# A first unit with an order of its own, and a running state kept whole: a gated-linear-attention and two mixture-of-experts layers on one core

## The chip, the cores and the metric

The kernel runs on one NeuronCore of one Trainium2 chip. The metric is device time in microseconds (us) of one execution; lower is better. Three executions of the kernel before took 754.09, 754.20 and 754.47 us, median 754.20 us.

## The reference

Three layers, one after the other. The attention keeps one 48x48 state for each of 2 batches x 8 heads; its decay `alpha` differs by row of the state and by position.

```python
# attention: q, k, v, alpha are [2, 8, 768, 48]
for t in range(S):
    state = alpha[:, :, t, :, None] * state + einsum('bhd,bhe->bhde', k[:, :, t], v[:, :, t])
    y[:, :, t] = einsum('bhd,bhde->bhe', q[:, :, t], state)
x = y.transpose(0, 2, 1, 3).reshape(1536, 384)
# first mixture: 4 experts, every row through all of them
for e in range(4):
    out += p[:, e:e + 1] * (relu(x @ w1[e]) @ w2[e])       # w1[e]: 384x1024, w2[e]: 1024x384
# second mixture: 8 experts, each row through the two that its noisy logits choose
```

## The kernel before

**Units and groups.** The 2 x 768 positions are cut into seven units (`sizes`: 128, 256, 256, 128, 256, 256, 256). Two heads form a pair (`p`, 96 of 128 partitions; a head has 48 rows at partition 0 or 64), and a chunk `c` is 128 positions. A group is two (pair, chunk) tiles side by side: two pairs of one chunk in a unit of 128, two chunks of one pair in a unit of 256. Groups are counted through all units by `k`: 0 and 1 are the first unit's, 2 to 5 the second's.

**Stages of a group.** `decays` transposes alpha on TensorE and makes with scans on VectorE the running products `A` and the reversed ones `F` (tile `suffix`). `keys` and `queries` transpose k and q and multiply them by `F` and `A`; ScalarE makes `G` from `K`. `keys_back` transposes `K` back, and ScalarE copies it out as `Kn`. `scores` multiplies G with Q into two PSUM banks, `sc0` and `sc1` (for two groups at once after the first unit), and VectorE masks each into `M`. `states` multiplies `Kn` with v into one bank, again `sc0`, and VectorE updates the state `St` from it: the result for a pair is 96x96, and only its two 48x48 blocks on the diagonal belong to the state. `outputs` adds the state's part and M's part in one PSUM bank; ScalarE copies it out rounded (`xh`), and VectorE takes the rest (`xl`). For the first unit the output goes to `x32` unsplit.

**Order.** `plan` gives each stage of a group a step: `base` plus an offset, where `base` rises by 2 for the first two groups and by 3 afterwards. Within a step the stages run by a fixed rank. Engines execute in the order in which the program was written. Wherever `IDLE` says so, `busy` puts matmuls of ones in front of a stage; nothing reads what they compute. The names `tr` (2 banks), `g` (4), `sc0` and `sc1` (1 each) are PSUM banks: a matmul that wants one waits until its last reader is done.

**Beside the attention** runs the first expert of the first mixture (`moe1(0, ...)`). `drive` takes a piece of it (`hidden` for one f, or two f of `product`) and then as many steps of the attention as keep both level. It starts with the first unit's 128 rows when the first `rows_at[0]` steps are written, which is 9. For these rows `hidden` uses whole float32 weights (L491, `raw` 4 to 7); afterwards each weight is a rounded part and a rest, with three matmuls (L495 to L497, L510 to L512). The rounded parts are made on ScalarE (L144) and the rests on GpSimd (L145), a group of weights in a piece.

**Loads** are issued by SyncE, in the order of the program, into one queue: the first unit's alpha, k and q in halves, its v, the second unit's alpha, k and q, weights 4 and 5, the second unit's v, weights 6 and 7, and then the second weights of the expert.

Of the kernel before, what the change touches and what calls it, by code (L numbers as in the profile page):

```python
# [28 lines left out]
def kernel(  # L29
# [203 lines left out]
    for i in range(2):  # L233
        t = apool.tile([P, BM, H, 2, D], F32, name=f"v{i}")
        nc.gpsimd.memset(t[:, :, :, 1, :], 0.0)
        V.append(t)
# [6 lines left out]
    def load_unit(u, names, p0=0, p1=HP):  # L243

        if u >= NU:
            return
        b, h0 = divmod(starts[u], S)
        hs = slice(2 * p0, 2 * p1)
        for nm in names:
            for c in range(sizes[u] // P):  # L250
                frm = src[nm][b, hs, h0 + c * P:h0 + (c + 1) * P, :].rearrange("h p d -> p h d")
                if nm == "v":
                    nc.sync.dma_start(V[u % 2][:, c, hs, 0], frm)
                    continue
                nc.sync.dma_start(inputs(nm, u)[:, c, hs, :D], frm)
# [9 lines left out]
    suffix = []  # L265
    for i in range(2):
        t = apool.tile([P, UM], F32, name=f"suffix{i}")
        nc.gpsimd.memset(t, 1.0)
        suffix.append(t)
    St = []  # L270
    for p in range(HP):
        t = apool.tile([P, BM + 1, 2 * D], F32, name=f"S{p}")
        nc.gpsimd.memset(t, 0.0)
        St.append(t)
# [4 lines left out]
    def attention(u):  # L279
# [8 lines left out]
        def slot(c):  # L288
            return (starts[u] // P + c) % (BM + 1)
# [17 lines left out]
        def decays(g):  # L307
            A = group(g, "A")
            st[g, "rc"] = rc = apool.tile([P, BM], F32, tag="rc", name="rc", bufs=3)
            st[g, "F"] = F = next(suffixes)  # L310
# [9 lines left out]
        def keys(g):  # L320
            K, G = group(g, "K", 2), group(g, "G")
            nc.vector.tensor_mul(K, transposed("k", g), st[g, "F"])
# [41 lines left out]
        def states(g):  # L364
# [4 lines left out]
            for i, p, c in updated(g):  # L369
                nc.tensor.matmul(t[:, i * 2 * D:(i + 1) * 2 * D].rearrange("x (j d) -> x j d", j=2), Kn[:, i, :],  # L370
                                 V[u % 2][:, c, 2 * p:2 * p + 2, 0, :], start=True, stop=True)
# [12 lines left out]

        def outputs(g):
            Q = st[g, "Q"]
            t = ps("g", 4)
            for i, (p, c) in enumerate(groups[g]):
                y = t[:2 * D, at(i)]
                inter = not (first and c == 0)  # L390
                if inter:
                    nc.tensor.matmul(y, St[p][:, slot(c), :], Q[:, at(i)], start=True, stop=False)  # L392
                two = V[u % 2][:, c].rearrange("x h k d -> x (h k d)")
                for j in range(2):
                    nc.tensor.matmul(y, two[:, (4 * p + j) * D:(4 * p + j + 2) * D], st[g, j][:, i, :],  # L395
# [21 lines left out]
            for y, r, d, to in pieces:  # L417
                nc.vector.tensor_sub(xl[r, d, to], y, xh.bitcast(F32)[r, d, to])  # L418
# [20 lines left out]
        def outputs_(g):  # L439
            outputs(g)  # L440
            if g == len(groups) - 1:
                load_unit(u + 2, "v")

        return len(groups), paired, (outputs_, states, keys, scores, keys_back, queries_, decays_), parted

    suffixes = itertools.cycle(suffix)

    rows_at = {}
    NEAR = 2

    IDLE = {(2, 0): 5, (1, 0): 5, (2, 1): 2, (1, 1): 4, (2, 2): 4, (1, 2): 2, (0, 0): 1, (0, 1): 1, (0, 2): 1}

    def plan():
        at = {}
        base = 0
        k = 0
        for u in range(NU):
            n, paired, stages, parted = attention(u)
            for g in range(n):
                near = k < NEAR  # L460
                offs = (5, 4, 1, 3, 3, 2, 0) if near else (7 if g % 2 or not paired else 9, 6, 1, 4, 3, 2, 0)
                for order, (stage, off) in enumerate(zip(stages, offs)):
                    at.setdefault(base + off, []).append((order, k, stage, g))
                end = base + (5 if near else 7)
                base += 2 if near else 3
                k += 1
            rows_at[u] = end + 2
            if u == 0:
                at.setdefault(end + 6, []).append((7, k, parted, 0))
# [4 lines left out]
    def stream():  # L474
        for i in range(max(steps) + 1):
            for order, k, f, g in sorted(steps.get(i, ()), key=lambda z: z[:2]):
                busy(IDLE.get((order, k), 0))
                f(g)
            yield
# [5 lines left out]
    def hidden(e, f, hx, lx, t0, n, H_):  # L485
        t = ps("g", 4)
        for kd in range(KD):
            if e == 0 and n == P:
# [13 lines left out]
        nc.vector.scalar_tensor_tensor(hl[:, :n], t[:, :n], 0.0, hh.bitcast(F32)[:, :n],  # L502
                                       op0=OP.max, op1=OP.subtract)
        H_[f] = (hh, hl)

# [10 lines left out]
    def moe1(e, t0, n, then=None):  # L516
        H_ = {}
        last = t0 + n == N
        for f in range(KF):
            hidden(e, f, xh, xl, t0, n, H_)  # L520
            if last and f % FG == FG - 1:
                W.done.add((e, 1, f // FG))
            yield
        if then is not None:
# [43 lines left out]
    psm = const.tile([P, NB], F32, name="psm")  # L568

    def probabilities():  # L570
        nc.vector.reduce_sum(psm, prob, axis=AX.X)
        nc.vector.tensor_scalar(psm, psm, 1e-9, None, op0=OP.add)
# [6 lines left out]
    for what in ("a", "k", "q", 4, 5, "v", 6, 7, 0, 1, "p", 2, 3):  # L579
# [18 lines left out]
    for _ in until(rows_at[0]):  # L598
        if now >= 15 and W.n_prep < 4:
            W.prep()  # L600
# [578 lines left out]
```

## Time and profile before

| | |
|---|---|
| median of three runs | 754.20 us |
| the profiled execution | 754.46 us, of which its span is 751.9 us |
| TensorE (PE) busy | 740.4 us, 98% |
| VectorE (DVE) busy | 358.0 us, 48% |
| ScalarE (ACT) busy | 246.2 us, 33% |
| GpSimd (POOL) busy | 163.4 us, 22% |
| chain of work that ended last | PE 92%, DVE 5% |

The span is what the trace covers; the 2.6 us beside it are the start and the end of the execution. Shares are over the whole span; the attention lasts for the first quarter of it, and there VectorE's share is far higher than in the table. A matmul's record runs to the modelled end of its pipeline, so two records overlap, and what the engine sustains is seen in the distance of their starts.

### The profile page before, as it was taken

How to read it: one execution, taken by the hardware profiler on the slowest of the kernel's cores; microseconds unless marked ns; L12 is line 12 of the kernel's file. 1: busy time of each engine (PE TensorE's matmuls, PEld its weight loads, DVE VectorE, ACT ScalarE, POOL GpSimd, SP SyncE). 2: the span in 40 equal slices, each digit the busy share in tenths (PEclk: the TensorE clock that was granted, in tenths of full speed). 3: DMA queues.
4: the chain of work that ended last, by engine and by line, in shares of the span. 5: the costliest groups of instructions: out<-in, count | busy, mean ns of one | idle time of the engine just before them, and what ended most of it. 6: DMA issues, size and time to landing. Idle time of an engine off the chain costs nothing.

```text
span 751.9 us, 11931 instructions
## 1 busy us (share of the span) xinstructions
PE 740.4 (98%) x4618; PEld 701.3 (93%) x4618; DVE 358.0 (48%) x868; ACT 246.2 (33%) x485; POOL 163.4 (22%) x177
## 2 busy tenths in 40 slices
PE   9999999999999999999999999999999999999997
PEld 5888999999898989989899999999999999999996
DVE  5888666664222122222212336367844564554551
ACT  2543323233312041210314314333534354444430
POOL 2440000001510032100134100011251524424331
PEclk9999999999999999999999999999999999999999
DMA  9945212100640012100114200011755554655620
GB/s 190 200 117 106 53 32 44 22 1 23 175 103 0 1 43 85 42 1 1 33 61 124 67 25 19 23 43 36 244 183 155 178 165 144 204 161 159 200 71 31
DMA packets 98254, 66.96 MB, mean 89 GB/s; under 512 B 57834, under 2 KB 94757, under 8 KB 98193
## 3 DMA queue, kind: packets, MB, share of 16 engines
q1 hardware_dynamic: 93168, 52.02, 25.8%
q0 software_dynamic: 5024, 14.13, 6.0%
q8 instruction: 38, 0.62, 0.3%
q14 instruction: 24, 0.19, 0.1%
HBM read 56.69 MB, written 9.82 MB: 88 GB/s over the span
## 4 chain that ended last, share of the span: by engine, by line
PE 92%; DVE 5%; ACT 1%; DMA 1%; issue 1%; POOL 0%; POOLq 0%; DVEq 0%
PE g L495 13%; PE g L496 13%; PE g L497 13%; PE g L510 10%; PE g L512 10%; PE g L511 10%; PE g L1019 3%; PE g L1021 3%; PE g L1020 3%; PE g L395 3%; PE tr L297 2%; PE sc L355 2%; PE tr L953 1%; PE g L192 1%; PE g L392 1%; PE sc L678 1%
## 5 line engine op out<-in xcount | busy, mean ns | idle before, releaser
L501 ACT ACTIVATE hh<-g 128x384 fp32r<-128x384 f32 (+8 forms) x200 | 96.7, 485 | 263.7 <-PE g L497 250.9
L502 DVE SCALAR_TENSOR_TENSOR hl<-g,hh 128x384 fp32r<-128x384 f32 (+8 forms) x200 | 109.1, 549 | 147.6 <-ACT hh L501 143.7
L510 PE MATMUL g<-w2h,hl 128*128 128x384 f32 x464 | 161.5, 348 | 0.0
L512 PE MATMUL g<-w2h,hh 128*128 128x384 f32 x464 | 156.4, 337 | 0.0
L511 PE MATMUL g<-w2l,hh 128*128 128x384 f32 x464 | 156.4, 337 | 0.0
L495 PE MATMUL g<-xh,w1l 128*128 128x512 f32 (+2 forms) x360 | 125.9, 350 | 0.0
L496 PE MATMUL g<-xl,w1h 128*128 128x512 f32 (+2 forms) x360 | 123.6, 343 | 0.1
L497 PE MATMUL g<-xh,w1h 128*128 128x512 f32 (+2 forms) x360 | 123.4, 343 | 0.0
L510 PEld LDWEIGHTS g<-w2h,hl 128*128 128x128 f32 x464 | 87.3, 188 | 1.0
L511 PEld LDWEIGHTS g<-w2l,hh 128*128 128x128 f32 x464 | 87.4, 188 | 0.3
L512 PEld LDWEIGHTS g<-w2h,hh 128*128 128x128 f32 x464 | 87.2, 188 | 0.0
L145 POOL TENSOR_TENSOR w1l<-raw,w1h 128x768 fp32r<-128x768 f32 x16 | 29.2, 1840 | 266.0 <-ACT w1h L144 266.0
L539 DVE SCALAR_TENSOR_TENSOR acc<-g,prob,acc 128x384 f32<-128x384 f32 x36 | 22.2, 618 | 116.9 <-PE g L512 116.9
L495 PEld LDWEIGHTS g<-xh,w1l 128*128 128x128 f32 x360 | 67.8, 188 | 6.0
L495 PE MATMUL g<-xth,w1l 128*128 128x256 f32 (+6 forms) x216 | 73.4, 340 | 0.0
L496 PEld LDWEIGHTS g<-xl,w1h 128*128 128x128 f32 x360 | 67.9, 189 | 5.8 <-DVE xl L418 0.3
L497 PEld LDWEIGHTS g<-xh,w1h 128*128 128x128 f32 x360 | 67.8, 188 | 5.7
L496 PE MATMUL g<-xtl,w1h 128*128 128x256 f32 (+6 forms) x216 | 71.3, 330 | 0.0
L497 PE MATMUL g<-xth,w1h 128*128 128x256 f32 (+6 forms) x216 | 71.4, 330 | 0.0
L144 ACT ACTIVATE w2h<-raw 128x768 fp32r<-128x768 f32 x44 | 36.8, 845 | 35.1 <-issue 23.0
L971 POOL DMA_INDIRECT out_dram<-yo,si_c x26 | 26.1, 1004 | 85.9 <-DVE yo L970 79.8
L1019 PE MATMUL g<-hh,w2l 128*128 128x432 f32 (+4 forms) x120 | 43.3, 361 | 0.0
(194 smaller groups left out, 1047.6 us busy)
## 6 DMA issues: line engine op xcount, KB each, us to landing
raw<-in_moe_w_dram SPq DMA_DIRECT2D x76, 384.0 KB
raw<-in_moe_w_dram SPq DMA_DIRECT2D x16, 288.0 KB
v<-in_v_dram SPq DMA_DIRECT2D x12, 192.0 KB
out_dram<-zero SPq DMA_DIRECT2D x1, 2304.0 KB
x2d<-acc SPq DMA_DIRECT2D x12, 192.0 KB
x_a<-in_alpha_dram SPq DMA_DIRECT2D x20, 96.0 KB
x_k<-in_k_dram SPq DMA_DIRECT2D x18, 96.0 KB
x_q<-in_q_dram SPq DMA_DIRECT2D x18, 96.0 KB
```

The costliest lines, as they stand in the source:

```text
L144: nc.scalar.activation(hi, r, AF.Copy)
L145: (nc.gpsimd if e < E1 or own else nc.vector).tensor_sub(lo, r, hi.bitcast(F32))
L495: nc.tensor.matmul(t[:, :n], wl, hx[:, kd, t0:t0 + n], start=(kd == 0), stop=False)
L496: nc.tensor.matmul(t[:, :n], wh, lx[:, kd, t0:t0 + n], start=False, stop=False)
L497: nc.tensor.matmul(t[:, :n], wh, hx[:, kd, t0:t0 + n], start=False, stop=(kd == KD - 1))
L501: nc.scalar.activation(hh[:, :n], t[:, :n], AF.Relu)
L502: nc.vector.scalar_tensor_tensor(hl[:, :n], t[:, :n], 0.0, hh.bitcast(F32)[:, :n], op0=OP.max, op1=OP.subtract)
L510: nc.tensor.matmul(t[:m, :DM], hl[:, o:o + m], wh, start=(f == 0), stop=False)
L511: nc.tensor.matmul(t[:m, :DM], hh[:, o:o + m], wl, start=False, stop=False)
L512: nc.tensor.matmul(t[:m, :DM], hh[:, o:o + m], wh, start=False, stop=(f == KF - 1))
L971: nc.gpsimd.indirect_dma_start(out=parts_of_out[s], out_offset=bass.IndirectOffsetOnAxis(ap=SLOT[e * SB + s][2][:n, e * SB + s:e * SB + s ...
L1019: nc.tensor.matmul(t[:, :n], wl, hh[:, :n], start=(f == 0), stop=False)
```

## The change

Five things change.

- The running state is kept whole. A tile `full` holds each pair's 96x96 result with its off-diagonal blocks. Each update is one instruction of 96 columns on all partitions instead of two of 48x48; the first chunk's is a copy on ScalarE. Two ScalarE copies then move the diagonal blocks into `St`, whose other blocks stay zero. These copies, and the rests `xl`, are put on a list (`later`) and written at the end of the step.
- `plan` has tables by stage: own steps and ranks for groups 0 and 1, and for the others `states` one step earlier, with a rank behind `queries`, and `scores` ahead of `keys`. In the first unit the making of the state (`keys_back`, `states`) comes after the outputs, and the transposes of the first q and the second alpha go to a `g` bank.
- `IDLE` holds 10 matmuls of ones instead of 25; the ten at the very start stay. The first expert starts after 5 steps instead of 9.
- Queues: weights 4 are loaded ahead of the second unit's k and q, and weights 6 ahead of its v, which so comes after three groups of weights instead of two. v is laid out as (head, zeros, head) for a pair, so that a load is two DMAs of half the size and the zeros are half as many. The third unit's v is loaded after the first unit's states.
- One `suffix` tile instead of two, `A` in two buffers instead of three; the sum of the probabilities gets its small constant from a tile. In `hidden`, for 128 rows, VectorE's `hl` is written after the attention's steps of that piece.

```diff
-                    nc.sync.dma_start(V[u % 2][:, c, hs, 0], frm)
+                    for j in range(2):
+                        nc.sync.dma_start(V[u % 2][:, c, p0:p1, 2 * j], frm[:, j::2])
...
-            t = ps("tr", 2)
+            t = ps("g", 4) if u == 0 and (nm, g) in (("q", 0), ("a", 1)) else ps("tr", 2)
...
-            for i, p, c in updated(g):
+            o = t[:, :BM * 2 * D].rearrange("x (i e) -> x i e", i=BM)
+            if first and UB == 1:
+                ps_ = slice(groups[g][0][0], groups[g][-1][0] + 1)
+                nc.scalar.activation(full[:, ps_, 0], o, AF.Copy)
+            else:
...
+                        prev = full[:, p, c - 1 if c else sizes[u - 1] // P - 1]
+                        nc.vector.scalar_tensor_tensor(full[:, p, c], prev, A[:, i * P + P - 1:i * P + P], o[:, i],
+                                                       op0=OP.mult, op1=OP.add)
...
+            def diagonal():
                 for j in range(2):
                     rows = slice(64 * j, 64 * j + D)
                     cols = slice(j * D, (j + 1) * D)
-                    o = t[rows, i * 2 * D + j * D:i * 2 * D + (j + 1) * D]
-                    to = St[p][rows, slot(c + 1), cols]
-                    if first and c == 0:
-                        nc.vector.tensor_copy(to, o)
-                    else:
-                        nc.vector.scalar_tensor_tensor(to, St[p][rows, slot(c), cols],
-                                                       A[rows, i * P + P - 1:i * P + P], o,
-                                                       op0=OP.mult, op1=OP.add)
+                    nc.scalar.activation(St[rows, ps_, new, cols], full[rows, ps_, :n, cols], AF.Copy)
+
+            later.append(diagonal)
...
-    IDLE = {(2, 0): 5, (1, 0): 5, (2, 1): 2, (1, 1): 4, (2, 2): 4, (1, 2): 2, (0, 0): 1, (0, 1): 1, (0, 2): 1}
+    NEAR = ({"decays": (0, 0), "keys": (0, 1), "queries": (0, 2), "scores": (1, 0), "outputs": (2, 0),
+             "keys_back": (4, 7), "states": (5, 5)},
...
+    ORDER = {"outputs": 0, "scores": 1, "keys": 2, "keys_back": 3, "queries": 4, "states": 5, "decays": 6}
...
+    IDLE = {("scores", 0): 2, ("outputs", 0): 3, ("scores", 1): 2, ("outputs", 1): 1, ("keys", 2): 2}
...
-        base = 0
+        base = 3
...
                 f(g)
+            while later:
+                later.pop(0)()
             yield
...
-    for what in ("a", "k", "q", 4, 5, "v", 6, 7, 0, 1, "p", 2, 3):
+    for what in ("a", 4, "k", "q", 5, 6, "v", 7, 0, 1, "p", 2, 3):
```

How the rows move shows at three places. The first is VectorE in the first unit, from the second group's scans on (`suffix`, `A`, `rc`), before:

```order
L315 SCALAR_TENSOR_TENSOR suffix_123<-tr,tri 128x127 x2
L317 SCALAR_TENSOR_TENSOR A<-tr,tri 128x128 x2
L318 RECIPROCAL rc<-A 128x2
L322 TENSOR_TENSOR K<-tr,suffix_123 128x256
L359 TENSOR_TENSOR M<-sc_226,tri 128x256
L359 TENSOR_TENSOR M<-sc_227,tri 128x256
L379 COPY S_125<-sc_248 48x48 x2
L379 COPY S_127<-sc_248 48x48 x2
L328 TENSOR_TENSOR Q<-tr,A 128x256
L315 SCALAR_TENSOR_TENSOR suffix_121<-tr,tri 128x127 x2
```

And after:

```order
L310 SCALAR_TENSOR_TENSOR suffix<-g,tri 128x127 x2
L312 SCALAR_TENSOR_TENSOR A<-g,tri 128x128 x2
L313 RECIPROCAL rc<-A 128x2
L354 TENSOR_TENSOR M<-sc_213,tri 128x256
L354 TENSOR_TENSOR M<-sc_214,tri 128x256
L317 TENSOR_TENSOR K<-tr,suffix 128x256
L323 TENSOR_TENSOR Q<-tr,A 128x256
L354 TENSOR_TENSOR M<-sc_252,tri 128x256
L354 TENSOR_TENSOR M<-sc_253,tri 128x256
L310 SCALAR_TENSOR_TENSOR suffix<-tr,tri 128x127 x2
```

The four copies into the state are gone, and both groups' masks now stand ahead of the second unit's first scans. The second place is ScalarE when the second unit begins, from that unit's first `G` on, before:

```order
L324 ACTIVATE G<-K,rc 128x128 x2
L342 ACTIVATE Kn<-tr 128x256
L411 ACTIVATE acc<-g 96x128
L411 ACTIVATE acc<-g 32x128
L342 ACTIVATE Kn<-tr 128x256
L324 ACTIVATE G<-K,rc 128x128 x2
L501 ACTIVATE hh<-g 128x128 x2
```

And after, where `full` and `S` are the new copies:

```order
L319 ACTIVATE G<-K,rc 128x128 x2
L337 ACTIVATE Kn<-tr 128x256
L525 ACTIVATE hh<-g 128x128
L370 ACTIVATE full<-sc_315 128x2x96
L337 ACTIVATE Kn<-tr 128x256
L387 ACTIVATE S<-full 48x2x48 x2
L525 ACTIVATE hh<-g 128x128
L337 ACTIVATE Kn<-tr 128x256
L370 ACTIVATE full<-sc_342 128x2x96
L387 ACTIVATE S<-full 48x2x48 x2
L525 ACTIVATE hh<-g 128x128
L319 ACTIVATE G<-K,rc 128x128 x2
```

The first unit's two states are now made here, between the second unit's first and second group. The third place is PE behind the scores of the second unit's first two groups, before:

```order
L355 MATMUL sc_442<-Q,G 128x128
L491 MATMUL g<-acc,raw 128x128 x3
L297 MATMUL tr<-ident,x_q_110 128x128 x2
L491 MATMUL g<-acc,raw 128x128 x3
L192 LDWEIGHTS ones_b
L192 MATMUL g<-ones_b 128x512
L392 MATMUL g<-Q,S_125 96x128
```

And after:

```order
L350 MATMUL sc_442<-Q,G 128x128
L293 MATMUL tr<-ident,x_k_108 128x128 x2
L293 MATMUL tr<-ident,x_q_110 128x128 x2
L365 MATMUL sc_471<-v_116,Kn 128x96 x2
L515 MATMUL g<-acc,raw 128x128 x3
L398 MATMUL g<-Q,S 96x128
```

The next state's matmul (L365), which needs the bank of `sc_441` back, now follows the scores after two pairs of transposes; before, it came after these outputs.

## Rows read from the trace of the kernel before

**Rows 1.** Busy time by stretch: PE, PEld, DVE, ACT, POOL (instructions), PE clock, DMA share, GB/s.
```profile
0.00:5.50 5.50, 4.37 (x12) 1.70 (x13) 0.46 (x3) 1.28 (x1) 4.75 (x20) 1.00 0.55 101
5.50:19.50 14.00, 12.99 (x91) 8.74 (x90) 10.39 (x36) 3.97 (x13) 0.68 (x3) 1.00 1.11 227
19.50:27.00 7.50, 6.98 (x65) 6.21 (x64) 6.38 (x22) 2.37 (x9) 0.00 (x0) 1.00 1.02 255
27.00:45.00 18.00, 17.16 (x144) 16.09 (x142) 15.07 (x47) 11.09 (x27) 13.64 (x8) 1.00 0.64 137
45.00:73.00 28.00, 26.33 (x220) 24.31 (x219) 22.82 (x68) 9.81 (x28) 1.81 (x1) 1.00 0.55 112
73.00:176.00 103.00, 103.00 (x806) 100.28 (x806) 67.45 (x192) 29.71 (x83) 0.00 (x0) 1.00 0.16 31
```

**Rows 2.** Chain of work in order of time, first 100 us: start, us, what.
```profile
1.13 4.39 PE g L192 x10
...
10.19 1.08 PE g L192 x5
...
12.61 0.87 PE g L395 x8
...
14.35 0.22 PE tr L297 x2
14.56 0.65 PE sc L355 x8
...
16.44 0.48 PE sc L370 x4
...
21.34 0.67 PE g L491 x6
```

**Rows 3.** Timeline of VectorE, 5 to 21 us: start, us, instruction, [idle before <-releaser].
```profile
5.86 0.73 DVE L315 TENSOR_TENSOR_SCAN suffix<-tr,tri 128x127 f32<-128x127 f32 x2 [3.63 <-PE tr L297]
...
7.76 0.42 DVE L328 TENSOR_TENSOR Q<-tr,A 128x256 f32<-128x256 f32 x1
...
10.14 0.74 DVE L359 TENSOR_TENSOR M<-sc,tri 128x256 f32<-128x256 f32 x2
...
19.48 0.73 DVE L315 TENSOR_TENSOR_SCAN suffix<-tr,tri 128x127 f32<-128x127 f32 x2
```

**Rows 4.** Timeline of ScalarE, 5 to 21 us.
```profile
7.77 0.69 ACT L324 ACTIVATE G<-K,rc 128x128 f32<-128x128 f32 x2 [5.67 <-DVE K L322]
...
10.86 0.36 ACT L342 ACTIVATE Kn<-tr 128x256 f32<-128x256 f32 x1
```

**Rows 5.** Timeline of PE, 17 to 28 us.
```profile
19.55 0.83 PE L491 MATMUL g<-acc,raw 128*128 128x128 f32 x6
...
27.19 0.38 PE L392 MATMUL g<-Q,S 128*96 128x128 f32 x2
```

**Rows 6.** Timeline of VectorE, 23 to 30 us.
```profile
24.20 0.73 DVE L315 TENSOR_TENSOR_SCAN suffix<-tr,tri 128x127 f32<-128x127 f32 x2
...
26.19 1.28 DVE L359 TENSOR_TENSOR M<-sc,tri 128x512 f32<-128x512 f32 x2
```

**Rows 7.** Groups by line and shape, first 100 us: busy us, mean ns | idle before.
```profile
L381 DVE SCALAR_TENSOR_TENSOR S<-S,A,sc 48x48 f32<-48x48 f32 x36 | 9.4, 261 | 0.8
...
L411 ACT ACTIVATE acc<-g 96x128 f32<-96x128 f32 x3 | 0.7, 270 | 4.4 <-PE g L395 4.4
```

**Rows 8.** A group of the page, whole span.
```profile
L539 DVE SCALAR_TENSOR_TENSOR acc<-g,prob,acc 128x384 f32<-128x384 f32 x36 | 22.2, 618 | 116.9 <-PE g L512 116.9
```

**Rows 9.** Timeline of PE, 31 to 51 us.
```profile
34.95 0.44 PE L297 MATMUL tr<-ident,x_k 128*128 128x128 f32 x2 [0.30 <-ACT Kn L342]
...
45.33 0.28 PE L495 MATMUL g<-xh,w1l 128*128 128x256 f32 x1
...
50.45 0.82 PE L355 MATMUL sc<-Q,G 48*128 48x128 f32 x9 [0.80 <-DVE S L381]
```

**Rows 10.** Timeline of all engines, 71 to 73 us.
```profile
72.86 0.44 PE L297 MATMUL tr<-ident,x_a 128*128 128x128 f32 x2 [0.46 <-DVE K L322]
```

More of the change, by code (lines that the diff above doesn't have):

```diff
@@ L262 @@
     W = Weights()
[L265 to L270, printed above, removed]
+    F = apool.tile([P, UM], F32, name="suffix")
+    nc.gpsimd.memset(F, 1.0)
+    full = apool.tile([P, HP, BM, 2 * D], F32, name="full")
+    St = apool.tile([P, HP, 4, 2 * D], F32, name="S")
     for p in range(HP):
-        t = apool.tile([P, BM + 1, 2 * D], F32, name=f"S{p}")
-        nc.gpsimd.memset(t, 0.0)
-        St.append(t)
+        nc.gpsimd.memset(St[:, p], 0.0)
     xh = xpool.tile([P, KD, N], F32R, name="xh")
@@ L440, in outputs_, with states_ @@
             outputs(g)
-            if g == len(groups) - 1:
+            if u and g == len(groups) - 1:
                 load_unit(u + 2, "v")
-        return len(groups), paired, (outputs_, states, keys, scores, keys_back, queries_, decays_), parted
-    suffixes = itertools.cycle(suffix)
-    rows_at = {}
-    NEAR = 2
-    IDLE = {(2, 0): 5, (1, 0): 5, (2, 1): 2, (1, 1): 4, (2, 2): 4, (1, 2): 2, (0, 0): 1, (0, 1): 1, (0, 2): 1}
+        def states_(g):
+            states(g)
+            if not u and g == len(groups) - 1:
+                load_unit(2, "v")
@@ new lines, in attention @@
+        return len(groups), UB, (outputs_, states_, keys, scores, keys_back, queries_, decays_), parted
+    rows_at = {}
+    later = []
+    NEAR = ({"decays": (0, 0), "keys": (0, 1), "queries": (0, 2), "scores": (1, 0), "outputs": (2, 0),
+             "keys_back": (4, 7), "states": (5, 5)},
+            {"decays": (0, 3), "keys": (1, 1), "queries": (1, 2), "scores": (2, 1), "outputs": (3, 7),
+             "keys_back": (5, 7), "states": (6, 5)})
+    FAR = ({"decays": 0, "keys": 1, "queries": 2, "keys_back": 3, "scores": 4, "states": 5, "outputs": 9},
+           {"decays": 0, "keys": 1, "queries": 2, "keys_back": 3, "scores": 4, "states": 5, "outputs": 7})
@@ L453, in plan @@
+    ORDER = {"outputs": 0, "scores": 1, "keys": 2, "keys_back": 3, "queries": 4, "states": 5, "decays": 6}
+    NAMES = ("outputs", "states", "keys", "scores", "keys_back", "queries", "decays")
+    IDLE = {("scores", 0): 2, ("outputs", 0): 3, ("scores", 1): 2, ("outputs", 1): 1, ("keys", 2): 2}
     def plan():
         at = {}
-        base = 0
+        base = 3
         k = 0
         for u in range(NU):
-            n, paired, stages, parted = attention(u)
+            n, UB, stages, parted = attention(u)
@@ L459, in plan @@
             for g in range(n):
[L460 to L465, printed above, removed]
+                for stage, nm in zip(stages, NAMES):
+                    step, order = NEAR[k][nm] if k < len(NEAR) else (base + FAR[g % 2][nm], ORDER[nm])
+                    at.setdefault(step, []).append((order, k, stage, g, nm))
+                    if nm == "outputs":
+                        end = step
@@ L475, in stream @@
         for i in range(max(steps) + 1):
-            for order, k, f, g in sorted(steps.get(i, ()), key=lambda z: z[:2]):
-                busy(IDLE.get((order, k), 0))
-                f(g)
+            for order, k, f, g, nm in sorted(steps.get(i, ()), key=lambda z: z[:2]):
+                busy(IDLE.get((nm, k), 0))
+                f(g)
+            while later:
+                later.pop(0)()
             yield
@@ L598 @@
     for _ in until(rows_at[0]):
-        if now >= 15 and W.n_prep < 4:
-            W.prep()
+        pass
     def n_moe(n):
```

51 lines of the change are left out of this document (34 added, 17 removed).

## The prediction

> **What bounds the kernel now.** I read first the page's chain of work, then busy time by stretch, then the chain and the engines' timelines up to 73 us. The chain is 92% PE. By stretch [rows 1], PE has no idle time from 73 to 176 us; before that it has some in every stretch: 14.00 - 12.99 = 1.01 us, then 0.52, 0.84 and 1.67, 4.04 us in all from 5.5 to 73. In the same stretches VectorE is busy 74 to 85% of the time, ScalarE at most 62%. So from 73 us on the kernel is as long as PE's list, and a change of the attention's order earns what it takes out of PE's row before: waits, and matmuls that nobody reads. Of these the chain holds 35 [rows 2]: ten from 1.13 us take 4.39, 0.44 each, which is the pace of the lower clock level (1.2 GHz), and later five take 1.08, 0.22 each, the pace of the upper (2.4 GHz). The granted clock is 1.00 in each of these stretches [rows 1]. The change takes out 15 of the later ones, 15 x 0.22 = 3.2 us, and keeps the first ten. With the idle time, 3.2 + 4.0 = 7.2 us is about the most that can be had; idle time counts from modelled ends, so a wait is a little longer than it says (six matmuls of L491 last 0.83 in the timeline, and 0.67 on the chain [rows 2, 5]).
>
> **The first unit (to 27 us).** The ten matmuls of ones stay in front, so VectorE's first scan stays at 5.86 [rows 3]. Up to its Q a group takes 1.90 for scans, reciprocal and K, and Q 0.42 [rows 3]: 8.18. Now nothing keeps the second group's scans, whose alpha has its own bank. VectorE's list goes on: scans, reciprocal and K 1.90, the first mask 0.74, Q 0.42: 11.24, with K done by 10.85. ScalarE's G takes 0.69 [rows 4], the second scores 0.65 [rows 2]: with hand-overs 12.5. The mask, 0.74, gives 13.3, the outputs on PE, 0.87 [rows 2], 14.2. VectorE does the second unit's scans, about 1.5 of that 1.90, before its last copies of the output (0.6, an estimate from the 0.74 for a pair of masks), so the first expert's row is whole by about 15.4, and PE reaches L491 at 15.2 to 15.5 instead of 19.55 [rows 5]: 4.2 us earlier.
>
> This lead does not last, because the first unit's two states now come behind it. ScalarE has then, from the second unit's K (15.9) on, in this order: G 0.69, Kn 0.36 [rows 4], a `hh` of 128 columns at about 0.27 (as L411, of that width [rows 7]), the first `full` (192 columns, 0.32 between L411's 0.27 for 128 and Kn's 0.36 for 256), Kn 0.36, two diagonal copies, `hh`, and so on. The second state's matmuls can't start before 15.9 + 0.69 + 0.36 + 0.27 + 0.32 + 0.36 = 17.9, PE has a second f (0.67) and a transposition ahead of them, and the alpha of the next group stands behind them: its scan comes at 19.3, where it came at 19.48 [rows 3]. Here VectorE's lead is used up. It comes back in part: scans, K and Q (1.90 + 0.42), two `hl` (0.3 each, 128 columns on the line used below for the update) and the new update (0.62) are 3.5 us of VectorE, and the scan after that starts near 22.8 instead of 24.20 [rows 6]. Carried on in the same way, with the masks of 1.28 for two groups [rows 6], PE starts the second unit's outputs at 26.5 instead of 27.19 [rows 5], and has by then done one f (0.67) and one state (0.48 [rows 2], 0.43 on a warm list) more. Lead: 0.7 + 0.7 + 0.4 = **1.8 us**. Ends: the six copies that ScalarE has between 16 and 20.5 at 0.35 (half of a G's 0.69, 128 columns from SBUF) instead of 0.27 (L411, 128 from PSUM [rows 7]) make it 0.5 later, and hand-overs as much again, 0.8; all 15 matmuls of ones gained in full make it 3.2.
>
> **Loads.** The queue is full in this time, DMA shares 1.11 and 1.02 [rows 1], so twelve more issues of half the size wait behind data and cost nothing of their own. The second unit's v now has 3,456 KB in front of it and in it (3.54 MB): 5.5 us at 101 GB/s is 0.56 MB, and the other 2.98 MB at 227 GB/s [rows 1] take 13.1 us: 18.7. It is wanted at about 21. Cost 0; at most some 1 us if the landing lags by three.
>
> **The update (all units).** It was four instructions of 0.261 [rows 7], 1.04 a group. At 96 columns I put one on the line between 48 columns (0.261) and 384 (0.618 [rows 8]), 0.31; two are 0.62, so VectorE saves 0.42 a group, 3.4 us over the eight groups to 73 us. ScalarE gains two copies a group, 0.27 to 0.35 each by the same two rows; I take 0.3 (96 columns, but from SBUF): three groups add 1.8 to its 11.09 of 18 us from 27 to 45, 72%.
>
> **27 to 45 us.** PE's list here is the old one without that f. Of the waits, 0.84 us, one is for ScalarE's Kn (0.30 at 34.95 [rows 9]). A new one arises twice: `states` follows the scores after two pairs of transposes, 0.22 each [rows 2], and wants the bank `sc0`, which VectorE releases after the first mask, half of 1.28 [rows 6]: 0.2 to 0.4 each. VectorE's relief is 3 x 0.42. I take a gain of **0.4 us**; ends -0.7 (new waits, none removed) and 0.8 (all removed).
>
> **45 to 73 us.** Two of the waits are named: the scores at 50.45 for the four updates (0.80 [rows 9]), and the alpha at 72.86 for a K that stood behind three `xl` (0.46 [rows 10]). Both causes go: `states` moves a step away from the next scores, with expert work between, and `xl` is written behind K. What is late next is PE's own list; `xl` itself is wanted only after two more stages and a product. Of 1.67 idle, somewhat more by starts, I take **2.0 us**; ends 1.0 and 2.3. After 73 us nothing: PE is full in both, and its real matmuls are the same.
>
> **Sum.** 1.8 + 0.4 + 2.0 = 4.2 us off the profiled execution's 754.46, 750.26; that execution lies 0.26 over the median 754.20, so **750.0 us**. Ends 0.8 - 0.7 + 1.0 = 1.1 and 3.2 + 0.8 + 2.3 = 6.3: 747.9 to 753.1.
>
> **Rivals.**
> *ScalarE takes VectorE's place.* It is in order, and the diagonal copies stand ahead of `hh` and of the next Kn, for which PE already waits once (0.30 [rows 9]). If every group to 45 us holds a Kn by its 0.6, five groups cost 3.0 of the 4.2: 753.0. For it: 72% and bursts. Against: from 45 to 73 ScalarE is 35% busy [rows 1].
> *The matmuls of ones were padding only.* Each one removed becomes a wait of its length, since PE waits for VectorE there, and the waits after 27 us are replaced by those for `sc0`: 754.2, give or take 0.8. Against: the second masks come 3 us earlier by VectorE's own list.
> *Every wait goes.* 7.2 us off: 747.0.
> *Slower: the clock falls.* PE is at the upper level when it has worked without a break through the ten ones [rows 2], and from 5.5 to 19.5 it is busy 12.99 of 14 us [rows 1], 23 ones among it. In the new order PE is idle from about 6.9 to 8.5, and again before each mask. If that takes the clock to 1.2 GHz, transposes, scores and outputs take twice as long, 1 us lost for each us of PE's work; it decides from 4.2 us of such work on. From 8.5 to 26.5 PE has 18 us less some 5 of waits and ones, 13 of it; if 10 of them run at the lower level and 3 of the loss fall into waits, 7 are lost: 754.2 - 4.2 + 7 = 757. Against: the longest break is under 2 us, and there is work on both sides of it. The Trainium skill's "TensorE: Matmul & The Clock Gate", in "Part 1: The HAM clock gate", says that activity releases the throttle and an idle PE goes back to half the clock; by that rule this order's breaks are the risk and the ones the insurance. By it the time is this rival's 757, by the rows alone the sum's 750.0. This trace shows the rise only, after the first ten; a fall it does not show.
>
> **Chances.** Forecast 0.62, ScalarE 0.14, padding 0.08, every wait 0.09, clock 0.07. A measurement of this kernel can tell about 0.2%, 1.5 us, from no change: faster is below 752.7, slower above 755.7. ScalarE's case reaches from 752 to 754, so about two thirds of it, 0.09, lie below 752.7. Faster 0.62 + 0.09 + 0.09 = 0.80; same 0.05 + 0.08 = 0.13; slower 0.07. The range 747.2 to 753.0 leaves out the clock, the padding and the far part of ScalarE's case, 0.2.
>
> **What would show it.** Right: L491's successor starts near 15.3 us, the second unit's second scan still near 19.3, its outputs near 26.5; no wait of the scores for the update; the new update at 0.31; PE full from 70 us on. Wrong: a granted clock under 1.00 in the first 30 us; PE waiting for Kn or `hh` behind the copies; `states` waiting for a mask by more than 0.4; a second v that lands after 21 us.

## The result

The changed kernel takes 760.09 us (median of six runs, 759.31 to 762.07), the kernel before 754.28 beside it: a ratio of 1.008, 95% interval 1.007 to 1.0091. The forecast was 750.0, with a range of 747.2 to 753.0, so the time went the other way by more than the gain that was expected. The profiled execution took 759.64 us with a span of 757.6, against 754.46 and 751.9 before; the spans differ by 5.7 us.

All of it arises before 52 us. The second phase of expert 0 (rows 128 to 383, the first `hidden` with `xh` and `w1l`) starts at 52.31 us, where it started at 45.33 [rows 9]: 7.0 later. From there to the end of the span the changed kernel needs 757.6 - 52.31 = 705.3 us, the kernel before 751.9 - 45.33 = 706.6. So 7.0 are lost and 1.3 come back.

The experiments below give the cause. Two things cost some 4 and some 5 us. A tile of four bytes moved the input tiles by 32 bytes, which made their loads slow; the forecast had the loads at cost 0. And four small instructions of VectorE now stand ahead of a pair of masks, and two of them are held up there by GpSimd; the forecast had the wait behind these masks at 0.2 to 0.4 us. With the tile gone and the four instructions moved, and the rest of the new order as it is, the kernel takes 750.63 us.

### The profile page after: what moved, and what is told of

Its sections match the earlier page's. It is cut to its first block, busy times and chain, and to the rows that moved or that the text cites. A ratio compares the mean times of both kernels' runs of the same rounds, so it can differ in the third digit from the quotient of the medians.

```text
span 757.6 us, 11938 instructions
## 1 busy us (share of the span) xinstructions
PE 741.8 (98%) x4603; PEld 704.7 (93%) x4603; DVE 348.8 (46%) x820; ACT 258.4 (34%) x535; POOL 162.9 (22%) x177
## 3 DMA queue, kind: packets, MB, share of 16 engines
q1 hardware_dynamic: 93360, 52.02, 26.5%
## 4 chain that ended last, share of the span: by engine, by line
PE 89%; DVE 4%; DMA 2%; SPq 1%; ACT 1%; POOL 1%; issue 1%; POOLq 0%; DVEq 0%
PE g L519 13%; PE g L520 13%; PE g L521 12%; PE g L540 11%; PE g L542 10%; PE g L541 10%; PE g L1052 3%; PE g L1054 3%; PE g L1053 3%; PE g L401 2%; PE tr L293 1%; PE tr L986 1%; PE sc L350 1%; SPq L255 1%; PE g L398 1%; PE sc L365 1%
## 5 line engine op out<-in xcount | busy, mean ns | idle before, releaser
L144 POOL TENSOR_TENSOR w1l<-raw,w1h 128x768 fp32r<-128x768 f32 x16 | 29.2, 1837 | 270.3 <-ACT w1h L143 270.3
L1004 POOL DMA_INDIRECT out_dram<-yo,si_c x26 | 26.1, 1004 | 88.5 <-DVE yo L1003 82.3
```

What stands on the lines that cost most here:

```text
L144: (nc.gpsimd if e < E1 or own else nc.vector).tensor_sub(lo, r, hi.bitcast(F32))
L1004: nc.gpsimd.indirect_dma_start(out=parts_of_out[s], out_offset=bass.IndirectOffsetOnAxis(ap=SLOT[e * SB + s][2][:n, e * SB + s:e * SB + s ...
```

## The profile of the changed kernel

Busy time by stretch, columns as in [rows 1]:

```profile
5.50:19.50 14.00, 12.17 (x89) 9.52 (x88) 8.74 (x28) 4.86 (x17) 0.15 (x2) 1.00 1.27 197
19.50:27.00 7.50, 5.25 (x31) 4.88 (x30) 3.82 (x13) 3.88 (x12) 0.03 (x1) 0.77 1.10 240
27.00:45.00 18.00, 14.47 (x121) 13.39 (x120) 15.23 (x41) 10.01 (x26) 9.98 (x6) 0.87 0.78 144
45.00:73.00 28.00, 27.17 (x222) 25.72 (x221) 17.77 (x51) 12.40 (x35) 5.44 (x3) 0.96 0.43 96
73.00:176.00 103.00, 103.00 (x807) 99.87 (x806) 66.45 (x179) 37.24 (x115) 0.00 (x0) 1.00 0.21 39
```

PE idles 2.25 us of the 7.5 up to 27 and 3.53 of the 18 up to 45; before it was 0.52 and 0.84. In the same three stretches the granted clock, 1.00 throughout before, is 0.77, 0.87 and 0.96. In the first row the DMA engines are busier than before, 1.27 against 1.11, and move less, 197 GB/s against 227.

What PE waited for from 2 to 73 us (line and what it waited for: us in all, times, longest):

```profile
PE sc L365 <- DVE M L354: 4.2, 3, 3.3
PE sc L365 <- DMA v<-in_v_dram: 1.7, 1, 1.7
PE sc L350 <- ACT G L319: 1.2, 1, 1.2
PE tr L293 <- DMA x_q<-in_q_dram: 0.6, 1, 0.6
PE tr L293 <- DVE A L312: 0.6, 1, 0.6
```

No wait is for ScalarE's copies of the state. Two are for loads, and the largest is that of the matmuls of `states` (L365) for a mask (L354). The same in PE's timeline, with the first of the second unit's outputs, which came at 27.19 before [rows 5]:

```profile
14.92 1.06 PE L515 MATMUL g<-acc,raw 128*128 128x128 f32 x6
16.85 0.33 PE L293 MATMUL tr<-ident,x_q 128*128 128x128 f32 x1 [0.57 <-DMA x_q<-in_q_dram]
...
23.45 0.71 PE L365 MATMUL sc<-v,Kn 128*128 128x96 f32 x2 [1.68 <-DMA v<-in_v_dram]
...
30.38 0.38 PE L398 MATMUL g<-Q,S 128*96 128x128 f32 x2
...
42.33 1.17 PE L365 MATMUL sc<-v,Kn 128*128 128x96 f32 x4 [3.34 <-DVE M L354]
...
43.67 0.52 PE L541 MATMUL g<-w2l,hh 128*128 128x384 f32 x1
43.99 0.52 PE L542 MATMUL g<-w2h,hh 128*128 128x384 f32 x1
```

Up to 15 us PE does what the forecast said; then it waits for q, for v, and at 39 us for a mask. After that wait the product's matmuls start 0.32 us apart (43.67, 43.99); ahead of it they were 0.17 apart (36.80, 36.97). The granted clock from 42 to 45 us is 0.50, its lower level.

Why the mask is late stands on VectorE and GpSimd:

```profile
37.96 0.19 DVE L605 TENSOR_REDUCE psm<-prob 128x12 f32<-128x48 f32 x1
38.26 1.62 DVE L606 TENSOR_TENSOR psm<-psm,tiny 128x12 f32<-128x12 f32 x1
39.91 0.23 DVE L607 RECIPROCAL psm<-psm 128x12 f32<-128x12 f32 x1
40.17 1.50 DVE L608 TENSOR_TENSOR prob<-prob,psm 128x48 f32<-128x48 f32 x1
41.59 1.27 DVE L354 TENSOR_TENSOR M<-sc,tri 128x512 f32<-128x512 f32 x2
```

```profile
38.03 1.81 POOL L144 TENSOR_TENSOR w2l<-acc,w2h 128x768 fp32r<-128x768 f32 x1 [1.65 <-ACT w2h L143]
...
39.80 1.80 POOL L144 TENSOR_TENSOR w1l<-raw,w1h 128x768 fp32r<-128x768 f32 x1
```

`probabilities` (L605 to L608) works on 12 and 48 columns. Its add and its product take 1.62 and 1.50 us, and each ends within 0.1 us of the end of one of GpSimd's weight parts, the rests of the weights that L144 makes (38.03 + 1.81 = 39.84; 39.80 + 1.80 = 41.60). The scores were done near 38.4, and the masks start at 41.59. In the kernel before, the masks stood ahead of `probabilities`:

```profile
37.30 1.28 DVE L359 TENSOR_TENSOR M<-sc,tri 128x512 f32<-128x512 f32 x2
38.49 0.19 DVE L571 TENSOR_REDUCE psm<-prob 128x12 f32<-128x48 f32 x1
38.72 0.17 DVE L572 TENSOR_SCALAR psm<-psm 128x12 f32<-128x12 f32 x1
38.93 0.23 DVE L573 RECIPROCAL psm<-psm 128x12 f32<-128x12 f32 x1
39.19 1.61 DVE L574 TENSOR_TENSOR prob<-prob,psm 128x48 f32<-128x48 f32 x1
```

Its product was held up too (1.61, beside a weight part that began at 38.92), but with no mask behind it.

## The experiments

Fifteen kernels. In the compiled program every tile has an address in a partition's memory; where an experiment moves tiles, the text tells by how much. In the kernel before, as compiled, `x_a`, `x_k` and `x_q` begin 64 bytes over a multiple of 256, and each row that a load writes into them is 192 bytes long, 256 apart. The changed kernel's `tiny`, one float a partition, takes 32 bytes, and everything allocated behind it moves by that.

### Taking `probabilities` and the tile apart

**Without `tiny`**, the constant added as before:

```
-    tiny = const.tile([P, 1], F32, name="tiny")
-    nc.gpsimd.memset(tiny, 1e-9)
...
-        nc.vector.tensor_add(psm, psm, tiny.to_broadcast([P, NB]))
+        nc.vector.tensor_scalar(psm, psm, 1e-9, None, op0=OP.add)
```

> The changed kernel with one instruction of `probabilities` as before: `tensor_scalar` with the constant 1e-9, no tile `tiny`. So both suspected causes in this instruction go at once: the two-SBUF-input add on VectorE beside GpSimd's weight parts, and the 32 bytes by which `tiny` moves every later tile. Theory A (the small tile's shift makes the loads slow, and the add holds up the mask): the second unit's v lands near 19 us as forecast, the mask before the states at 42 us is not held up, the clock does not fall; 750 to 752 us. Theory B (the add as in A, but the loads are slow through the new order of the queue: weight 4 ahead of k and q, 6 ahead of v, v in halves): v still lands past 22 us with a break of PE before the states, the mask free; 755 to 757. Theory C (PE's breaks without the fifteen ones take the clock down, wherever they come from): granted clock under 1.00 before 50 us, 757 to 760.

Measured: 755.3 us, ratio 1.0013 (1.0005 to 1.0022). No wait for a load is left, and the second unit's outputs start at 26.60 instead of 30.38. But the masks were as late as ever. VectorE and GpSimd in it:

```profile
34.41 1.69 DVE L604 TENSOR_SCALAR psm<-psm 128x12 f32<-128x12 f32 x1
36.13 0.23 DVE L605 RECIPROCAL psm<-psm 128x12 f32<-128x12 f32 x1
36.40 1.50 DVE L606 TENSOR_TENSOR prob<-prob,psm 128x48 f32<-128x48 f32 x1
37.81 1.28 DVE L354 TENSOR_TENSOR M<-sc,tri 128x512 f32<-128x512 f32 x2
```

```profile
34.26 1.81 POOL L144 TENSOR_TENSOR w2l<-acc,w2h 128x768 fp32r<-128x768 f32 x1 [1.64 <-ACT w2h L143]
36.03 1.80 POOL L144 TENSOR_TENSOR w1l<-raw,w1h 128x768 fp32r<-128x768 f32 x1
```

The add with the constant, one input, is held just as long (1.69) as that with two. So theory A was right on the loads and wrong on the add: it is not the new instruction that holds the masks, but where the four stand. For that reason A's 750 to 752 us was missed. The sign of theory C came too, a clock under 1.00 before 50 us (0.81 from 27 to 45); but the clock stays at 1.00 up to 37.3 us and falls in the wait for the mask, and not at a break that the missing ones leave.

**`tiny` at 64 bytes**, 16 columns of which one is read, meant to bring tiles back to multiples of 64.

> The changed kernel with `tiny` 16 columns wide, of which one is read, so that later tiles stand at multiples of 64 bytes again; the add of two SBUF inputs stays. Theory A: v lands near 19 us, no break before the states at 23 us, but the add still takes about 1.6 us and the mask behind it is late if GpSimd's weight part falls on it: a PE break of 1 to 3.5 us near 38 to 42; 753 to 756. Theory B: loads as late as in the changed kernel, 759 to 760. If the add is not what holds the mask: near 750 with an add of 0.2.

Measured: 761.7 us, ratio 1.0092 (1.0076 to 1.0107), loads as late as in the changed kernel; theory B came nearer than A. Multiples of 64 are not what counts; theory A needed another rule for the address.

**The tile alone**, `tensor_scalar` back and `tiny` kept unused:

> The changed kernel with `tensor_scalar` back, but the unused tile `tiny` kept, so that the 32-byte shift stays and the add goes. Theory A: the second unit's v lands past 22 us and PE stands still before the states near 23 us as in the changed kernel; the break near 40 is gone; 754 to 757. Theory B: the same as without the tile, 755 to 757 both, so it is the difference to that kernel that counts: A wants 3 us or more between them, B under 1.

Measured: 759.38 us, 1.0073 (1.006 to 1.0086), 4.1 more than without the tile. A's difference, not B's; the time lies over A's 754 to 757, since the masks are still held (PE waits 2.28 us for them at 40.78).

**The tile in the kernel before**, unused, nothing else changed:

> The kernel before with an unused tile `tiny` of 4 bytes a partition added at the same place (its memset on GpSimd too), nothing else. Theory A: the loads of the first 20 us run at the slower packet rate of the changed kernel, v lands past 20 us instead of 18.4; since v is wanted later there than in the changed kernel, 754 to 757. Theory B: landings and time unchanged, 754.3 within 0.5.

Measured: 757.09 us, 1.0044 (1.0032 to 1.0057), where theory B had no change. The kernel before, too, loses 2.6 us by four bytes that nobody reads, in its order of the queue. PE waits in it for k of the third unit, 1.48 us at 35.77, which it did not before. So B, the new order of the queue, is not needed to explain the slow loads.

### The place of `probabilities`, address against memset, and the clock

**`probabilities` later.** In the kernel without `tiny`, the call moves from ahead of the first phase's product to behind it, just ahead of the line that multiplies by `prob`:

```
-        if then is not None:
-            then()
...
+            if i == 0 and weigh is not None:
+                weigh()
```

> The kernel without `tiny` (755.3 us) with the four instructions of `probabilities` moved behind the first phase's product, just ahead of the first use of `prob`; nothing else. Theory lock (the two of them that want both SBUF inputs or the fast mode stand still while GpSimd forms a weight part, and hold the masks by 3.4 us): the masks come at their scores, PE's break of 3.5 us at 35 us shrinks to under 0.9, the granted clock stays at 1.00 from 27 to 45 us; 3.0 of wait and about 3 of clock go, 748.5 to 750.5 us. Theory bank (the states wait for the bank `sc0` whatever stands ahead of the masks, since a pair of masks takes 1.28): the break stays above 2 us, 753 to 755.

Measured: **750.63 us**, ratio 0.9946 (0.9932 to 0.9959). PE's stretches in it:

```profile
5.50:19.50 14.00, 12.54 (x92) 9.99 (x91) 8.92 (x29) 5.05 (x18) 0.11 (x1) 1.00 1.10 228
19.50:27.00 7.50, 6.74 (x63) 6.03 (x63) 7.09 (x23) 5.13 (x16) 2.78 (x2) 1.00 1.04 266
27.00:45.00 18.00, 17.81 (x150) 17.12 (x149) 12.94 (x41) 12.15 (x31) 10.84 (x7) 1.00 0.72 150
45.00:73.00 28.00, 27.18 (x231) 25.23 (x231) 22.38 (x65) 11.28 (x34) 1.83 (x1) 1.00 0.53 109
```

Idle time from 27 to 45 is 0.19 us, and the clock stays at 1.00. Where GpSimd is at rest, the add and the product of `probabilities` take 0.17 and 0.21:

```profile
45.03 0.17 DVE L606 TENSOR_SCALAR psm<-psm 128x12 f32<-128x12 f32 x1
...
45.50 0.21 DVE L608 TENSOR_TENSOR prob<-prob,psm 128x48 f32<-128x48 f32 x1
```

The theory of the bank falls, but for a rest of 0.19 where the 3.34 was; the time is 0.1 us over the upper end of the other theory.

**A tile that nothing touches**, 4 bytes a partition, in the kernel without `tiny`: the same list of instructions at other addresses.

> The kernel without `tiny` (755.3 us) with an unused tile of 4 bytes a partition that no instruction touches: every later tile moves by 32 bytes, and the list of instructions is the same. Theory address: packets of 192 bytes of the second unit take 28 ns instead of 15, v lands past 22 us, 758 to 760 us. Theory memset (the extra GpSimd instruction, not the address, delays or slows the loads): 15 ns, v by 19.5, 755 to 756.

**The memset without the tile:** `nc.gpsimd.memset(psm, 1e-9)` at the place of that of `tiny`.

> The kernel without `tiny` with an extra GpSimd memset of `psm` at the place of that of `tiny`, and no extra tile: no address moves. Theory memset: packets of 192 bytes at 28 ns, v past 22 us, 758 to 760. Theory address: as without it, v by 19.5, 755 to 756.

Measured: 758.87 us (1.0067, 1.0051 to 1.0082) and 755.6 us (1.0015, 1.0006 to 1.0024), with packets of 26.1 and 15.6 ns. It is the address, and not the memset.

**PE's break filled** with matmuls of ones, in the kernel without `tiny`: `IDLE` gets `("states", 5): 15`.

> The kernel without `tiny` (755.3 us) with fifteen matmuls of ones ahead of the states of the second unit's last group, where PE stands still for 3.5 us behind the masks: the wait stays, PE is busy in it. Theory clock (the break takes the clock to its lower level for some 7 us, which costs about 3): clock 1.00 from 27 to 45 us, the masks no earlier, 752 to 753 us. If the clock falls for another reason: 755 or more, since the ones only replace idle time.

Measured: 753.74 us, 0.9992 (0.9983 to 1.0001). The row from 27 to 45 us of the kernel without `tiny`, and then PE's break and the same row with the ones:

```profile
27.00:45.00 18.00, 14.66 (x105) 14.00 (x104) 12.12 (x32) 9.70 (x25) 8.99 (x6) 0.81 0.54 109
```

```profile
35.09 3.40 PE L191 MATMUL g<-ones_b 128*128 128x512 bf16 x15
38.51 0.69 PE L365 MATMUL sc<-v,Kn 128*128 128x96 f32 x4
...
27.00:45.00 18.00, 17.98 (x143) 15.43 (x141) 13.93 (x38) 10.81 (x27) 10.35 (x6) 1.00 0.58 119
```

The states start when they did (38.55 without the ones), so no wait is gone; the clock alone is back. The second phase starts at 46.17 instead of 48.86, and at 43.08 with `probabilities` later: of 5.8 us of delay the clock made 2.7, the wait 3.1. At the end of the kernel 1.6 of the clock's part is left, 755.3 against 753.74, less than the 2 to 3 expected.

### What it is in the address

In the kernel with `probabilities` later and without `tiny`, an unused tile ahead of the pools moves everything behind it: `pad = const.tile([P, n], F32, name="pad")` with n of 32, 48, 64 and 128, that is 128, 192, 256 and 512 bytes.

> The kernel with `probabilities` later and without `tiny` (750.6 us), with an unused tile of 128 bytes a partition ahead of the pools, which moves every later tile by 128 bytes: `x_a`, `x_k`, `x_q` and `v` from 64 to 192 over a multiple of 256. Shifts of 32 and 64 were slow. Theory 256 (a row of 192 bytes that crosses a multiple of 256 is slow): slow, 28 ns a packet, 753 to 755 us. Theory 128 (a row has to start at 64 over a multiple of 128): fast, 750.6. Theory place (only where the tiles stand in the kernel before is fast): slow.

> The same with a tile of 192 bytes: the rows of 192 bytes start at multiples of 256. Theory 256: fast, 15 ns, 750.6 us. Theory 128: slow, 753 to 755. Theory place: slow.

> The same with a tile of 256 bytes: the rows start at 64 over a multiple of 256 as in the kernel before, 256 bytes further on. Theory 256 and theory 128: fast, 15 ns, 750.6 us. Theory place, or a period of 512 bytes or more: slow, 28 ns, 753 to 755.

> The same with a tile of 512 bytes: as the kernel before, 512 bytes further on. Theories 256 and 128, and a period of 512 bytes: fast, 750.6 us. Theory place or a longer period: slow, 753 to 755.

Measured: 754.61 (1.0004, 0.9994 to 1.0015), 750.41 (0.995, 0.9933 to 0.9966), 751.0 (0.9956, 0.9939 to 0.9974) and 750.4 us (0.9953, 0.9936 to 0.9969). Slow, fast, fast, fast: only "a row that crosses a multiple of 256 is slow" foretold all four. The stretch of the loads with 128 bytes and with 192:

```profile
5.50:19.50 14.00, 12.66 (x92) 9.97 (x91) 8.80 (x29) 5.06 (x18) 0.12 (x1) 1.00 1.26 196
19.50:27.00 7.50, 5.14 (x30) 4.55 (x28) 4.32 (x15) 3.67 (x12) 0.57 (x1) 0.78 1.06 239
```

```profile
5.50:19.50 14.00, 12.57 (x92) 10.03 (x91) 8.92 (x29) 5.05 (x18) 0.11 (x1) 1.00 1.07 234
19.50:27.00 7.50, 6.74 (x63) 6.02 (x63) 7.09 (x23) 5.13 (x16) 2.77 (x2) 1.00 1.01 264
```

More busy DMA engines, fewer bytes, and behind that the clock, as in the changed kernel.

Then the tile only ahead of the attention's own pool (32 bytes; the weights' `raw` stays), and only ahead of `v`:

```
+    pad = apool.tile([P, 8], F32, name="pad")
```

> The kernel with `probabilities` later and without `tiny` (750.6 us), with an unused 32-byte tile at the head of the attention's own pool: `x_a`, `x_k`, `x_q` and `v` move by 32 bytes (their rows cross multiples of 256), the weights' `raw` stays. Theory rows (it is the 192-byte rows of the inputs that pay for the crossing): slow as with the 128-byte shift of everything, 28 ns a packet, 753.5 to 755 us. Theory weights (the 1024-byte rows of `raw` lose the rate, and the inputs only queue behind them): 15 ns, 750.6.

> The same tile put behind the `x` tiles, so that `v` alone moves by 32 bytes: of its rows of 192 bytes six of eight cross a multiple of 256 instead of four. The rows of `x_a`, `x_k` and `x_q` cross none. Theory rows: only the packets of v are slower, 21 to 24 ns instead of 19, v lands under 1 us later, which a v landing at 19.5 and wanted near 21 covers: 750.4 to 751.2 us. If the distance of `v` to the `x` tiles counts: 753 or more.

Measured: 755.2 us (1.0009, 0.9996 to 1.0023) and 750.25 (0.9942, 0.9925 to 0.9958). The waits for loads from 2 to 80 us, first with the inputs moved, then with `v` alone:

```profile
PE sc L366 <- DMA v<-in_v_dram: 2.0, 1, 2.0
...
PE tr L294 <- DMA x_q<-in_q_dram: 0.4, 1, 0.4
```

```profile
PE sc L366 <- DMA v<-in_v_dram: 0.6, 1, 0.6
```

The weights' address is out of it: `raw` stood still, and the loads were slow. `v` is waited for because it queues behind `x_k` and `x_q`, more than by its own rows: moved alone, it is waited for by 0.6 us instead of 2.0, though the expectation had no wait there. Both times lie up to 0.2 us outside what the theory of the rows gave.

The trace has a start and a duration for every packet. The mean time of a packet of 192 bytes while the second unit's k and q are loaded (4096 packets), by where a row of `x` starts over a multiple of 256:

| kernel | row starts at | crosses | ns a packet | time, us |
|---|---|---|---|---|
| before | 64 | no | 15.4 | 754.28 |
| before with the tile | 96 | yes | 28.4 | 757.09 |
| changed | 96 | yes | 27.7 | 760.09 |
| changed, `tiny` at 64 bytes | 128 | yes | 27.4 | 761.7 |
| changed, `tiny` at 256 bytes (below) | 64 | no | 15.4 | 755.73 |
| changed, constant's add, `tiny` unused | 96 | yes | 27.6 | 759.38 |
| without `tiny` | 64 | no | 15.5 | 755.3 |
| same, 4 bytes that nothing touches | 96 | yes | 26.1 | 758.87 |
| same, the memset alone | 64 | no | 15.6 | 755.6 |
| same, PE's break filled | 64 | no | 16.1 | 753.74 |
| `probabilities` later | 64 | no | 16.4 | 750.63 |
| same, 128 bytes | 192 | yes | 27.5 | 754.61 |
| same, 192 bytes | 0 | no | 15.3 | 750.41 |
| same, 256 bytes | 64 | no | 15.8 | 751.0 |
| same, 512 bytes | 64 | no | 15.4 | 750.4 |
| same, inputs by 32 | 96 | yes | 27.5 | 755.2 |
| same, `v` by 32 | 64 | no | 16.6 | 750.25 |

Last, **the changed kernel with `tiny` 256 bytes wide**, so that no row of `x` crosses, the add and the place of `probabilities` being the changed kernel's:

> The changed kernel with `tiny` 64 columns (256 bytes) wide: rows cross as little as in the kernel before, while the add of two SBUF inputs and the place of `probabilities` ahead of the masks are the changed kernel's. Theory place (it is where `probabilities` stands that holds the masks, and the constant's add was held in the same way): 755.3 us as with the constant, PE's break of 3.3 to 3.5 us near 35 us, clock under 0.9 from 27 to 45. Theory add (the add of two SBUF inputs has a price of its own): 756.5 or more.

Measured: 755.73 us, 1.0017 (1.0007 to 1.0026), an interval that overlaps with that of the kernel without `tiny` (1.0005 to 1.0022). PE's wait for the mask is the same 3.3. The add costs nothing of its own that these runs can tell.

The two effects side by side, in us:

| | rows of `x` cross nothing | rows cross |
|---|---|---|
| `probabilities` ahead of the masks | 755.3 (constant), 755.73 (add) | 758.87, 759.38 (constant), 760.09 (add) |
| `probabilities` behind them | 750.63 | 754.61, 755.2 |

The addresses cost 3.6 to 4.6, the place 3.7 to 5.5, and both together 9.5: to within 1 us they add. How much of the addresses' cost is the clock's was not tried by itself; in the two kernels at 758.87 and 759.38 the clock does not fall behind the wait for `v`, and the addresses cost 3.6 and 4.1 there.

## The prediction, step by step

**What bounds the kernel:** right. PE is full from 73 us on in the changed kernel too (103.00 of 103), and from the start of the second phase to the end of the span the changed order needs 705.3 us (705.5 with `probabilities` later), the one before 706.6.

**The first unit:** right to 0.4 us, where the loads leave it alone. In the kernel with `probabilities` later, on PE and then on VectorE:

```profile
14.92 1.06 PE L515 MATMUL g<-acc,raw 128*128 128x128 f32 x6
...
26.59 0.38 PE L398 MATMUL g<-Q,S 128*96 128x128 f32 x2
...
43.08 0.28 PE L519 MATMUL g<-xh,w1l 128*128 128x256 f32 x1
...
49.67 0.69 PE L365 MATMUL sc<-v,Kn 128*128 128x96 f32 x4 [0.68 <-DVE M L354]
```

```profile
19.41 0.73 DVE L310 TENSOR_TENSOR_SCAN suffix<-tr,tri 128x127 f32<-128x127 f32 x2 [2.03 <-PE tr L293]
...
22.87 0.73 DVE L310 TENSOR_TENSOR_SCAN suffix<-tr,tri 128x127 f32<-128x127 f32 x2 [0.27 <-PE tr L293]
```

The successor of L491 starts at 14.92 (15.2 to 15.5 forecast), the second unit's scan at 19.41 (19.3), the next at 22.87 (22.8), the outputs at 26.59 (26.5), and by then PE has done one f and one state more, as forecast. The lead of 1.8 and the 0.4 after it make 2.2 at the second phase's start; it is 45.33 - 43.08 = 2.25.

**The loads, cost 0: this step failed.** It took the rate of the kernel before, 227 GB/s, as given. The changed kernel has 197, because the diff's smallest line moves every input row across a multiple of 256 bytes. The bytes were counted right: in the kernel without `tiny` the last packet of the second v starts at 18.55 us (18.7 forecast), and no wait for v is left. With the shift v is waited for by 1.68 us and q by 0.57, and behind the break in PE the clock is down (0.77). Three of the text's own signs for wrong came: a second v after 21 us, a granted clock under 1.00 in the first 30 us, and `states` waiting for a mask by more than 0.4.

**27 to 45 us, a gain of 0.4: this step failed too.** It listed what PE waited for and the new wait of the states for `sc0`, at 0.2 to 0.4 each, from half of a pair of masks. It did not look at what stands ahead of the masks. The new order, read from the program, had it in plain sight. VectorE's list at that place, before and after:

```
L359 TENSOR_TENSOR M<-sc_622,tri 128x512
L359 TENSOR_TENSOR M<-sc_623,tri 128x512
L571 TENSOR_REDUCE psm<-prob 128x12
L572 TENSOR_SCALAR psm<-psm 128x12
L573 RECIPROCAL psm<-psm 128x12
L574 TENSOR_TENSOR prob<-prob,psm 128x48
```

```
L605 TENSOR_REDUCE psm<-prob 128x12
L606 TENSOR_TENSOR psm<-psm,tiny 128x12
L607 RECIPROCAL psm<-psm 128x12
L608 TENSOR_TENSOR prob<-prob,psm 128x48
L354 TENSOR_TENSOR M<-sc_617,tri 128x512
L354 TENSOR_TENSOR M<-sc_618,tri 128x512
```

The function was not costed at all, since in the trace of before nobody waited for it; and its product's 1.61 us on 48 columns was there to be read. As a wait of the states it took 3.34 instead of 0.2 to 0.4, and with the clock 3.7 to 5.5 us of the time. Without it the new wait is 0.19 (twice, at 25.37 and 35.41), at the low end of the term.

**The update:** right. At 96 columns one takes 0.309 us (0.31 forecast), and a copy of the diagonal 0.281 (0.3).

**45 to 73 us, a gain of 2.0:** mis-sized. From the second phase's start to the end of the span the kernel with `probabilities` later gains 706.57 - 705.52 = 1.05 us, the lower end. The two waits named did go; one for `sc0`, 0.68 at 49.67, came for them, and PE's idle time is 0.82 where 0 was hoped for.

**The sum:** 4.2 us. With the two unseen effects removed the medians differ by 754.39 - 750.63 = 3.8, within the range on record. The spans differ by 751.9 - 748.6 = 3.3, of which 2.25 arise up to the second phase and 1.05 behind it. But for the two effects the mechanism of the order was read rightly; for the kernel as it stands the forecast was wrong, by these two, at 9.5 us together.

**The rivals.** ScalarE did not take VectorE's place: its copies of the diagonal take 0.57 a pair, and PE waits for a Kn once, 0.55 us at 16.95 in the kernel with `probabilities` later. The padding was more than padding, for the same lead of 2.25. Nor did every wait go: in that kernel PE still idles 3.2 us from 5.5 to 73 us, against 4.0 before. The rival of the clock, at 0.07, came nearest to the time (757) but not by its mechanism: it put the fall between 8.5 and 26.5 us for breaks that the missing ones leave, and with `probabilities` later the clock is 1.00 through all of it, with PE waiting 0.9 us for G; it falls behind the waits for v and for the mask. So its nearness is luck. Its part was measured at 1.6 us of the time in the one case that was tried. The prediction says that the trace of the kernel before shows no fall of the clock; it shows one at its very end, 0.51 from 749.4 us on, where no matmul runs.

## What to carry to other kernels

A change in allocation is a change: before a forecast, compare the addresses of the tiles that loads fill, and keep rows so that they cross no multiple of 256 bytes that they need not cross (shown here for rows of 192 bytes). Where an order changes, read what now stands ahead of each instruction that another engine waits for, untouched lines among it, and look for short VectorE work whose duration in the trace is far over its size: here it showed what GpSimd held. A break of PE costs more than its length where the clock falls behind it (here 2.7 us beside the wait's 3.1 up to the second phase), so the cause of the break is worth more than its row says.

## What the runs showed of the hardware

**Rows that cross a multiple of 256 bytes.** Packets of 192 bytes that all cross one took 26 to 28 ns, and 15 to 17 where none does, and the engines then moved about 850 packets a us instead of 1,000 to 1,200. Starts of 0 and 64 over a multiple were fast, and of 96, 128 and 192 slow; rows of another length were not tried. The cost shows only where the queue is full: the first unit's rows take 15 to 19 ns in all these kernels, also where they cross (the k and q of the first unit do so in each). Why that is so was not tried. The Trainium skill's "DMA: Bandwidth & Descriptors", under "How a descriptor splits into AXI transactions", says that a transaction has to start at a multiple of 256 bytes, so that the first one of a descriptor that starts off such a multiple begins at the multiple below it; it tells it of reads. An estimate by that page's rule is one transaction for a row of 192 bytes that crosses no multiple, and two for one that crosses. The runs agree in direction, and show it for where the row is written.

**VectorE beside GpSimd.** An add with a constant on 12 columns took 0.17 us alone and 1.69 beside a weight part, a product of two inputs on 48 columns 0.21 and 1.50; the reduce and the reciprocal between them were not held (0.19, 0.23). The Trainium skill's "SBUF — State Buffer", under "Who interferes with whom", says that GpSimd shares a pair of ports with VectorE, that the one that comes second is blocked for the whole instruction, and that this meets operations with two inputs from SBUF, where GpSimd reads SBUF too, and those of a two-port mode, which `tensor_scalar` can enter. The trace agrees in each of these four.

**The clock.** It fell to its lower level (granted 0.50, 1.2 GHz, from 23.5 to 26.5 us in the changed kernel) in or behind waits of PE for v of 1.18 us (`tiny` at 64 bytes), 1.68 (changed kernel), 1.79 (128 bytes) and 2.04 (inputs moved), and for the mask of 2.28 to 3.35. It did not fall behind waits for v of 1.25 us (4 bytes that nothing touches) and of 1.77 in the changed kernel with the constant's add and `tiny` unused, whose row says so:

```profile
19.50:27.00 7.50, 5.17 (x50) 4.55 (x49) 5.05 (x18) 4.39 (x14) 0.53 (x1) 1.00 1.04 217
```

So much the same wait cost the clock in one run and not in another; why, these runs don't settle. Waits of up to 1.40 us for G near 8 us, and the break of 3.3 us with ones in it, left the clock at 1.00. The Trainium skill's "TensorE: Matmul & The Clock Gate", in "Part 1: The HAM clock gate", says that an idle PE goes back to half the clock; the runs agree in that.
